# Weights by GpSimd's DMA queue, product operands in half tiles, and a reordered tail in a gated FNet/SwiGLU mix

## The chip, the cores and the metric

The kernel runs on one core of a Trainium2 chip, as one program and one launch. The metric is the device time in microseconds, from a handful of executions of the same program; the text gives the median and the range of the runs shown. The profile is of one execution. Its engines are TensorE (PE, with the weight loads as PEld), VectorE (DVE), ScalarE (ACT), GpSimd (POOL) and SyncE (SP). SP computes nothing here: it issues most of the DMAs, one after the other, and an issue that has to wait for a buffer holds up every issue behind it. GpSimd issues DMAs too, in the same in-order manner, between its few computations.

## The reference, cut to what matters

```python
def reference(x, dft_seq_re, dft_seq_im, dft_hid_re, dft_hid_im, w1, w3, w2, gate_w):
    g = sigmoid((x * gate_w).sum(-1, keepdims=True))
    # A: FNet mixing, the real part of a DFT along hidden and sequence
    a_re, a_im = x @ dft_hid_re.T, x @ dft_hid_im.T
    a = dft_seq_re @ a_re - dft_seq_im @ a_im
    # B: SwiGLU
    b = (silu(x @ w1) * (x @ w3)) @ w2
    return g * a + (1 - g) * b
```

The sequence has 2048 tokens, the hidden width D is 512 and the inner width F is 1376. All inputs are fp32. The DFT matrices are inputs, too: the kernel may use their symmetries only after it has compared the given matrices with themselves (a row against a representative row), and it holds a general path for matrices that lack them.

## The kernel before, in words

**Precision.** Every operand is split into a high and a low part (fp32r tiles of twice the size): `high` (L113) is a ScalarE copy that rounds, `low` (L116) a VectorE subtraction that keeps the rest. `mm3` (L127) multiplies high by high, high by low and low by high, so each product is three passes.

**Start, 0 to 17 us.** The first products go through four PSUM banks named C.

**Gate stage, 17 to 213 us.** The work is cut into items n = 0..21. An item is one chunk of 128 columns of F (11 chunks; the last is partial) for one half of the tokens: chunks 0 to 8 with the first half are n = 0..8, chunks 9 and 10 with both halves are n = 9..12, and chunks 0 to 8 with the second half are n = 13..21. `WSET[n]` names the weight set of an item; n = 9 and 10 share set 9, n = 11 and 12 share set 10, and the sets 11 to 19 are the chunks 0 to 8 a second time. In a Strassen-like form each item takes seven products of six matmuls each, into PSUM banks X, Y and Z. In program order an item issues X with operand 4 (and continues a bank that was started three items earlier), Z with 5, the first product of the item three ahead (`LOOK = 3`), X with 3, Z with 2, the second product of the item three ahead, and X with 6. The last three items have five products, as nothing is left to start.

For a weight set there are four tiles. `ws` holds the raw weights, loaded by `load_w` (L198) from `w13` (1024 columns wide, or 768 where the set's sums are not made again). `wa` (three operands) is split out of `ws` in the item four before its use. `wu` is four sums out of `ws` (`sums_wb`, L220 to L223). `wb` (four operands, 1 MB) is split out of `wu` by `high_wb` and `low_wb`, used in the item after, and for the chunks 0 to 8 written to DRAM (`wbsp`) by GpSimd's queue (L238), from where the sets of the second round read it back (`load_wb`, L205, SP's queue) instead of making it anew.

ScalarE's part of an item is: copy of X out of PSUM (`h`, L343), copy of Z (`u`, L347), copy of the early X (`s`, L261), the high parts, a silu (`h`, L376) and a silu on the gate (L279). VectorE adds X, Z and Y into these copies (L356, L364, L365, L380, L275), makes the sums and the low parts. The product h is written to DRAM (`hs`, L305) by GpSimd's queue.

**Work spread over the items.** Between these, the program places tasks from one queue by a table: `work(eng, us)` takes tasks of engine "D" (VectorE) or "A" (ScalarE) for about that many us at one of five points of an item (`early`, `ahead`, `second`, `mid`, `at_end`). Most of the tasks are the comparisons of the DFT matrices: a tile `t` of 128 by 1024 is loaded (L698), VectorE adds or subtracts the representative (`differ`, L703 to L709), ScalarE sums up the absolute values (`add_up`, L714), and the buffer is free again. Their loads stand on SP's queue in program order among the loads of `ws` and `wb`.

**H stage, 213 to 327 us.** The product with `w2` over 22 steps: `hr` is read back, split to `ht` (the `high_h`, `low_h` and `high_w2`, `low_w2` of the first steps stand in item 21), and eight PSUM banks are summed over 11 chunks, twice.

**DFT stage, 327 us to the end.** The products O1 (two), O2 and E2 (two) are made, split to `z_O` and `z_E`, and used by ten units Y0 to Y9 of 12 matmuls each (four O1 units, two O2 units, four E2 units). VectorE forms r out of Y, gate and B's part (L1271), four operations in an O1 or O2 unit and two in an E2 unit, and `out` is stored. Between them `verdict` (L543, L545) turns the sums of the comparisons into flags, a matmul with ones adds them up over the partitions in a PSUM pair named `count` (L548), and L549 writes a word that every engine loads at the end (L1285) to branch to the general path.

The order of all of this is written out by hand: the schedule is manual, and within an engine the instructions run in program order.

Of the kernel before, what the change touches and what calls it, by code (L numbers as in the profile page):

```python
# [30 lines left out]
def fnet_swiglu_gate_kernel(  # L31
# [108 lines left out]
    wbsp = dram.tile([NC, P, 2, 4, 256], F32, tag="wbsp", name="wbsp")  # L140
# [60 lines left out]
    def load_wb(w, spare=False):  # L201

        WB[w] = (parts(f"wb{w}") if spare else
                 wbp.tile([P, 2, 4, 256], F32R, tag="wb", name=f"wb{w}"))
        nc.sync.dma_start(WB[w].bitcast(F32), wbsp[SETS[w]])  # L205
# [10 lines left out]
    def sums_wb(w):  # L216
# [3 lines left out]
        nc.vector.tensor_add(u[:, 0], r[:, 3], r[:, 2])  # L220
        nc.vector.tensor_sub(u[:, 1], u[:, 0], r[:, 0])
        nc.vector.tensor_sub(u[:, 2], r[:, 0], r[:, 3])
        nc.vector.tensor_sub(u[:, 3], r[:, 1], u[:, 1])  # L223

    def wb_parts(w):
        return [(flat(WB[w][:, 0, i:j]), flat(WB[w][:, 1, i:j]), flat(WU[w][:, i:j]))
                for i, j in ((0, 2), (2, 4))]

    def high_wb(w):
        WB[w] = wbp.tile([P, 2, 4, 256], F32R, tag="wb", name=f"wb{w}")  # L230
        for v in wb_parts(w):
            high(*v[::2])

    def low_wb(w):
        for v in wb_parts(w):
            low(*v)
        if w < K:
            nc.gpsimd.dma_start(wbsp[w], WB[w].bitcast(F32))  # L238

    def prod(ps, n, wi, xi, start, chain=False):  # L240
        w = WSET[n]
        w, wi = (WA[w], wi) if wi < 3 else (WB[w], wi - 3)
        x = xo_at(ITEMS[n][1], xi)
        for q in range(2):
            sl = slice(q * P, (q + 1) * P)
            mm3(ps, w[:, 0, wi, sl], w[:, 1, wi, sl], x[:, 0, q, :], x[:, 1, q, :],
# [69 lines left out]

    def gate_up(n):
# [10 lines left out]
        if nw in WB or nw == 0:  # L328
            nw = None
        elif back(nw):  # L330
            load_wb(nw)
# [21 lines left out]
        if nw is not None and n > 1:  # L353
            high_wb(nw)
        prod(x, n, 3, 3, False, True)
# [4 lines left out]
        if nw is not None:  # L360
            low_wb(nw)
        run(mid, n)
# [23 lines left out]
    load_w(0, 0, 1)  # L386
# [1145 lines left out]
```

## Time and profile before

| what | us |
|---|---|
| median of 3 runs (lowest to highest) | 364.74 (364.08 to 364.97) |
| the profiled execution | 364.39 |
| its span, first to last instruction | 362.6 |
| PE busy | 350.2 (97%) |
| DVE busy | 310.8 (86%) |
| ACT busy | 234.4 (65%) |
| POOL busy | 60.6 (17%) |
| mean granted TensorE clock | 0.996 |

The profiled execution took 1.79 us more than its span, which lies before the first and behind the last instruction, and 0.35 us less than the median. In the views, a row of a timeline gives start and duration in us, engine, line, operation, tile written and tiles read, and in square brackets the idle time ahead of it with the instruction that ended it. A group of PE's matmuls has a modelled end, so the distance from one row's start to the next is the better measure of what a product takes. In the rows of waits the three numbers are the total in us, how often, and the longest. Buffer numbers are left out in the trace: `ws` is any `ws` tile.

### The profile page before, as it was taken

To read this page: it belongs to the slowest core of one execution; us is meant where nothing else is said; L and a number is where in the kernel's file an instruction comes from. 1 tells how busy PE (TensorE), PEld (TensorE's weight loads), DVE (VectorE), ACT (ScalarE), POOL (GpSimd) and SP (SyncE) were. 2 spreads that over 40 slices of the span, in tenths; PEclk is the share of its full clock that TensorE was granted. 3 is DMA by queue.
4 is the path that set the end of the run, shared out by engine and by line. 5 is a ranking of instruction groups with operands and counts; after the bars stand their busy time and mean duration, and the time that the engine had idled before them with its cause. 6 is when DMAs were issued, how large, how long until landed. Compare 5 with 4: busy or idle time off the path is not lost.

```text
span 362.6 us, 5086 instructions
## 1 busy us (share of the span) xinstructions
PE 350.2 (97%) x1720; PEld 303.5 (84%) x1720; DVE 310.8 (86%) x433; ACT 234.4 (65%) x394; POOL 60.6 (17%) x96
## 2 busy tenths in 40 slices
PE   7999999999999999999999989999999999999993
PEld 3888888888888777788888868888888888889983
DVE  3999989999779788778887679989889799997693
ACT  4876766656647577754433579354688999888630
POOL 0001212211110111111111553419011020000000
PEclk9999999999999999999999999999999999999998
DMA  7638967757537679999899519974969999996065
GB/s 243 277 136 308 360 243 263 288 217 275 202 118 246 229 216 409 405 360 417 311 389 304 193 71 377 409 281 139 349 223 338 398 410 409 411 407 235 2 261 207
DMA packets 32064, 102.77 MB, mean 283 GB/s; under 512 B 5666, under 2 KB 5923, under 8 KB 29988
## 3 DMA queue, kind: packets, MB, share of 16 engines
q1 hardware_dynamic: 27204, 81.96, 61.9%
q0 software_dynamic: 4832, 20.46, 14.5%
q8 instruction: 14, 0.23, 0.3%
q14 instruction: 14, 0.11, 0.1%
HBM read 77.76 MB, written 24.65 MB: 282 GB/s over the span
## 4 chain that ended last, share of the span: by engine, by line
PE 79%; DMA 6%; DVE 6%; ACT 5%; issue 2%; SPq 0%; DVEq 0%; ACTq 0%
PE H L127 31%; PE X L127 23%; PE Z L127 11%; PE Y L127 6%; DMA ws<-w 5%; PE C L127 3%; PE O L127 3%; DVE r L1271 2%; ACT t L714 2%; DMA xs_B<-xt 1%; PE Y L1246 1%; PE E L127 1%; DVE wb L116 1%; DVE t L703 1%; DVE h L364 1%
## 5 line engine op out<-in xcount | busy, mean ns | idle before, releaser
L127 PE MATMUL H<-w2t,ht 128*128 128x512 f32 (+1 forms) x528 | 114.1, 379 | 0.0
L127 PEld LDWEIGHTS H<-w2t,ht 128*128 128x128 f32 (+1 forms) x528 | 99.8, 189 | 14.2
L127 PE MATMUL X<-xo,wb 128*128 128x512 f32 x378 | 89.7, 381 | 3.5 <-DVE u L356 1.5
L127 PEld LDWEIGHTS X<-xo,wb 128*128 128x128 f32 x378 | 70.9, 189 | 16.1 <-ACT h L343 3.1
L714 ACT ACTIVATE t<-t 128x1024 f32<-128x1024 f32 (+1 forms) x68 | 67.5, 995 | 3.6 <-DVE t L703 2.3
L305 POOL DMA_DIRECT2D hs<-h x36 | 19.5, 543 | 103.2 <-DVE h L365 75.6
L703 DVE TENSOR_TENSOR t<-t,rep 128x1024 f32<-128x1024 f32 x28 | 33.2, 1217 | 0.0
L127 PE MATMUL X<-xo,wa 128*128 128x512 f32 x126 | 30.9, 380 | 0.2 <-DVE wa L116 0.2
L127 PE MATMUL Y<-xo,wa 128*128 128x512 f32 x126 | 30.6, 379 | 0.0
L127 PE MATMUL Z<-xo,wb 128*128 128x512 f32 x126 | 30.6, 379 | 0.0
L127 PE MATMUL Z<-xo,wa 128*128 128x512 f32 x126 | 30.6, 379 | 0.0
L356 DVE TENSOR_TENSOR u<-u,X 128x512 f32<-128x512 f32 x21 | 14.4, 685 | 17.5 <-PE X L127 12.9
L376 ACT ACTIVATE h<-X 128x512 f32<-128x512 f32 x21 | 12.4, 593 | 25.1 <-PE X L127 21.7
L113 ACT ACTIVATE wa<-ws 128x768 fp32r<-128x768 f32 (+2 forms) x21 | 17.0, 807 | 18.0 <-DMA ws<-w 12.4
L705 DVE TENSOR_TENSOR t<-t,rep 128x1024 f32<-128x1024 f32 x24 | 28.2, 1217 | 0.0
L113 ACT ACTIVATE ht<-hr 128x1024 fp32r<-128x1024 f32 x19 | 20.0, 1051 | 11.2 <-PE H L127 8.9
L127 PEld LDWEIGHTS X<-xo,wa 128*128 128x128 f32 x126 | 23.7, 189 | 3.9 <-DVE wa L116 0.6
L127 PEld LDWEIGHTS Y<-xo,wa 128*128 128x128 f32 x126 | 23.8, 189 | 3.4
L127 PEld LDWEIGHTS Z<-xo,wb 128*128 128x128 f32 x126 | 23.8, 189 | 3.4
L127 PEld LDWEIGHTS Z<-xo,wa 128*128 128x128 f32 x126 | 23.8, 189 | 3.4
L116 DVE TENSOR_TENSOR wa<-ws,wa 128x768 fp32r<-128x768 f32 (+1 forms) x22 | 19.3, 880 | 7.1 <-ACT wa L113 6.9
L116 DVE TENSOR_TENSOR ht<-hr,ht 128x1024 fp32r<-128x1024 f32 x19 | 23.1, 1218 | 1.3 <-ACT ht L113 1.2
(198 smaller groups left out, 487.2 us busy)
## 6 DMA issues: line engine op xcount, KB each, us to landing
t<-wt SPq DMA_DIRECT2D x60, 512.0 KB, 9.4
hr<-hs SPq DMA_DIRECT2D x19, 512.0 KB, 7.2
hs<-h POOLq DMA_DIRECT2D x36, 256.0 KB, 4.7
wbsp<-wb POOLq DMA_DIRECT2D x8, 1024.0 KB, 4.7
wb<-wbsp SPq DMA_DIRECT2D x8, 1024.0 KB, 9.3
ws<-w SPq DMA_DIRECT2D x11, 512.0 KB, 5.1
xr<-xw SPq DMA_DIRECT2D x8, 512.0 KB, 11.5
xs_B<-xt SPq DMA_DIRECT2D x7, 512.0 KB, 5.8
```

The source lines that it names most:

```text
L113: nc.scalar.activation(hi, src, AF.Copy)
L116: nc.vector.tensor_sub(lo, src, hi.bitcast(F32))
L127: nc.tensor.matmul(ps.rearrange("p (n a) -> p n a", a=2), u, turns(v)[:, some], **kw)
L305: nc.gpsimd.dma_start(hs[c][:, b * TB : (b + 1) * TB], h)
L356: nc.vector.tensor_add(u4, u4, x)
L364: nc.vector.tensor_add(u2, u2, z)
L376: nc.scalar.activation(g1, x, AF.Silu)
L703: nc.vector.tensor_sub(t, t, r)
L705: nc.vector.tensor_add(t, t, r)
L714: nc.scalar.activation(t[:, :n], t[:, :n], AF.Abs, accum_out=acc[:, i : i + 1])
L1246: nc.tensor.matmul(to, u[i], v[j], start=n == k == 0, stop=n == len(terms) - 1 and k == 2, skip_group_check=True)
L1271: nc.vector.scalar_tensor_tensor(rv[:, :, h], src, g_pos[:, k : k + 1], nv[:, :, h], op0=ALU.mult, op1=ALU.add)
```

## The change

1. **`load_w` by GpSimd's queue.** The sets 6 to 19 are loaded by GpSimd's queue, at points that a small table `NEXT_W` fixes: right behind `low_wb` of the set four before (in program order), or at the start of an item for the last ones. The sets 0 to 5 stay on SP.
2. **`wb` in two half tiles.** Half 0 holds the operands 4 and 5, half 1 the operands 3 and 6; each has two buffers, and `wbsp` is written and read by halves of 512 KB. For the sets that are read back, half 0 is loaded two items ahead, and half 1 at the start of the item ahead. The first sum made is now the one of `wu`'s third column block. The items 19 and 20 take a full spare tile as before.
3. **The table.** In the items 10 and 12 (where the next item has another set) the `mid` point places no VectorE task; before it placed one.
4. **Item 21.** `low_h(0)` and `low_w2(0)` move from `second` to `mid`, which stands behind the addition to u4.
5. **The tail.** E2's first product stands ahead of unit 0 and its second ahead of unit 4, where both stood ahead of unit 0. One `add_up` fewer stands between the two O1 products; `verdict` moves from unit 2 to behind unit 3's r; the sum of the flags goes to a corner of unit 7's own PSUM pair, and the word is written behind unit 7's r.

```diff
-    wbsp = dram.tile([NC, P, 2, 4, 256], F32, tag="wbsp", name="wbsp")
+    wbsp = dram.tile([NC, 2, P, 2, 2, 256], F32, tag="wbsp", name="wbsp")
-    def load_w(w, lo=0, hi=4):
+    def load_w(w, lo=0, hi=4, by=nc.gpsimd):
         if lo == 0:
             WS[w] = f4_a.tile([P, 4, 256], F32, tag=f"f4_{4 + w % (LOOK + 1)}", name=f"ws{w}")
-        nc.sync.dma_start(WS[w][:, lo:hi].rearrange("p a n -> p (a n)"),
-                          w13[SETS[w], :, lo * 256 : hi * 256])
+        by.dma_start(WS[w][:, lo:hi].rearrange("p a n -> p (a n)"), w13[SETS[w], :, lo * 256 : hi * 256])
+    def new_wb(w, half):
+        t = wbp.tile([P, 2, 2, 256], F32R, tag=f"wb{half}", name=f"wb{half}_{w}")
+        WB.setdefault(w, {})[half] = t
+        return t
+    def load_wb(w, half):
+
+        nc.sync.dma_start(new_wb(w, half).bitcast(F32), wbsp[SETS[w], half])
...
     def low_wb(w):
-        for v in wb_parts(w):
-            low(*v)
-        if w < K:
-            nc.gpsimd.dma_start(wbsp[w], WB[w].bitcast(F32))
+        for half in range(2):
+            low(*wb_parts(w, half))
+            if w < K:
+                nc.gpsimd.dma_start(wbsp[w, half], WB[w][half].bitcast(F32))
...
+    NEXT_W = {}
+    for w in range(LOOK + 3, len(SETS)):
+        v = w - LOOK - 1
+        at = (WSET.index(v) - LOOK, 0) if back(v) else (WSET.index(v) - 1, 1)
+        NEXT_W.setdefault(at, []).append(w)
...
-        if nw in WB or nw == 0:
+        if nw == 0 or nw == WSET[n] or len(WB.get(nw, ())) == 2:
             nw = None
         elif back(nw):
-            load_wb(nw)
+            load_wb(nw, 1)
             nw = None
...
-        elif wa not in WS:
-            load_w(wa, 0, 3 if back(wa) else 4)
-        w = WSET[min(n + LOOK + 2, last)]
-        if w - LOOK - 1 >= NC + 1 and w not in WS and w not in WA:
+        for w in NEXT_W.get((n, 0), ()):
             load_w(w, 0, 3)
...
             high_wb(nw)
+        if n + 2 < NI - 3 and back(WSET[n + 2]):
+            load_wb(WSET[n + 2], 0)
         prod(x, n, 3, 3, False, True)
         nc.vector.tensor_add(u4, u4, x)
...
             low_wb(nw)
+        for w in NEXT_W.get((n, 1), ()):
+            load_w(w, 0, 3 if back(w) else 4)
         run(mid, n)
...
-            do(mid, n, work, "D", 1.7 if n >= SPARE[1] else 1.3)
+            do(mid, n, work, "D", 1.7 if n >= SPARE[1] else 1.3 if WSET[n] == WSET[n + 1] else 0.0)
...
-        do(at_end if m else second, NI - 1, low_h, m)
-        do(at_end if m else second, NI - 1, low_w2, m)
+        do(at_end if m else mid, NI - 1, low_h, m)
+        do(at_end if m else mid, NI - 1, low_w2, m)
...
-                work("A", 2.4)
+                work("A", 1.2 if p else 2.4)
...
+    even(0)
     for u, (kind, za, zb, n, swap) in enumerate(UNITS):
+        if u == 4:
+            even(1)
         ps = next_two(f"Y{u}")
+        if u == 7:
+            sum_flags(ps)
...
         if u == 2:
             work_until(set(range(n_late)))
+        if u == 3:
             verdict()
-        if u == 6:
-            verdict_end(next_two("count"))
+        if u == 7:
+            see_flags(ps)
```

`even(p)` is the product E2 of half p and its split, which stood in a loop ahead of the units before.

How the instructions stand, at three places.

SP's queue in the items 8 to 12 before, where the loads of the comparison tiles `t`, of the weights `ws` and of `wb` take turns:

```order
L198 DMA ws12_1024<-w13 128x768
L698 DMA t38_1044<-wt 128x1024
L698 DMA t39_1046<-wt 128x1024
L698 DMA t40_1106<-wt 128x1024
L198 DMA ws13_1111<-w13 128x768
L698 DMA t41_1129<-wt 128x1024
L698 DMA t42_1181<-wt 128x1024
L198 DMA ws14_1190<-w13 128x768
```

and GpSimd's queue now, where the weights stand between the stores of `wb` (`wbsp`) and of h (`hs`); SP's queue keeps the comparison tiles:

```order
L248 DMA wbsp_97<-wb0_8_841 128x1024
L248 DMA wbsp_97<-wb1_8_843 128x1024
L198 DMA ws12_856<-w13 128x768
L320 DMA hs_96<-h7_805 128x512 x2
L198 DMA ws13_939<-w13 128x768
L320 DMA hs_96<-h8_891 128x512 x2
L320 DMA hs_96<-h9_972 128x512 x2
L198 DMA ws14_1094<-w13 128x768
```

The loads of the weights moved from between the comparison tiles to between the stores, and they are issued one to three items earlier in program order.

VectorE at the end of the gate stage before (item 21: `u4_21` is added to, and `ht0` and `w2t0` are the first operands of the H stage):

```order
L380 TENSOR_TENSOR h20_1794<-h20_1794,u4_20_1795 128x512
L116 TENSOR_TENSOR ht0_1864<-h19_1744,ht0_1864 128x1024
L116 TENSOR_TENSOR w2t0_1866<-w2r0_1791,w2t0_1866 128x512
L356 TENSOR_TENSOR u4_21_1845<-u4_21_1845,X21_1693 128x512
L364 TENSOR_TENSOR h21_1844<-h21_1844,Z21_1843 128x512
```

and now:

```order
L402 TENSOR_TENSOR h20_1822<-h20_1822,u4_20_1823 128x512
L376 TENSOR_TENSOR u4_21_1868<-u4_21_1868,X21_1718 128x512
L116 TENSOR_TENSOR ht0_1888<-h19_1770,ht0_1888 128x1024
L116 TENSOR_TENSOR w2t0_1890<-w2r0_1819,w2t0_1890 128x512
L386 TENSOR_TENSOR h21_1867<-h21_1867,Z21_1866 128x512
```

The two low parts moved from ahead of the addition to u4 to behind it.

VectorE in the DFT stage now, from the second half of O1's first split on (before, all the comparisons stood ahead of s0, and the four low parts of E2 ahead of r0):

```order
L116 TENSOR_TENSOR z_O10_3025<-s0_3021,z_O10_3025 128x1024
L736 TENSOR_TENSOR t62_2945<-t62_2945,rep3_2573 128x1024
L736 TENSOR_TENSOR t63_3005<-t63_3005,rep3_2573 128x1024
L1235 TENSOR_TENSOR s1_3069<-e1_3068,O1_1_3029 128x512
L1236 TENSOR_TENSOR s1_3069<-e1_3068,O1_1_3029 128x512
L116 TENSOR_TENSOR z_O11_3073<-s1_3069,z_O11_3073 128x1024
L116 TENSOR_TENSOR z_O2_3076<-O2_3077,z_O2_3076 128x1024
L116 TENSOR_TENSOR z_E2_3119<-E2_0_3120,z_E2_3119 128x258 x2
L1303 SCALAR_TENSOR_TENSOR r0_3153<-Y0_3140,tail_93,nb0_2933 128x2x128 x4
```

and on ScalarE, where E2's second split now stands behind seven sums of the comparisons (four before, which stood behind that split):

```order
L113 ACTIVATE z_E2_3119<-E2_0_3120 128x258 x2
L741 ACTIVATE t57_2887,tail_93<-t57_2887 128x1024
L741 ACTIVATE t58_2890,tail_93<-t58_2890 128x1024
L741 ACTIVATE t59_2902,tail_93<-t59_2902 128x1024
L741 ACTIVATE t60_2915,tail_93<-t60_2915 128x1024
L741 ACTIVATE t61_2925,tail_93<-t61_2925 128x1024
L741 ACTIVATE t62_2945,tail_93<-t62_2945 128x1024
L741 ACTIVATE t63_3005,tail_93<-t63_3005 128x1024
L113 ACTIVATE z_E2_3119<-E2_1_3225 128x258 x2
```

Two comparisons moved in between the two splits of O1, and E2's second split moved behind all sums.

More of the change, by code (lines that the diff above doesn't have):

```diff
@@ L193, in back, with load_kept @@
         return w >= NC and SETS[w] > 0
-    def load_w(w, lo=0, hi=4):
+    def load_w(w, lo=0, hi=4, by=nc.gpsimd):
         if lo == 0:
             WS[w] = f4_a.tile([P, 4, 256], F32, tag=f"f4_{4 + w % (LOOK + 1)}", name=f"ws{w}")
-        nc.sync.dma_start(WS[w][:, lo:hi].rearrange("p a n -> p (a n)"),
-                          w13[SETS[w], :, lo * 256 : hi * 256])
[L201 to L205, printed above, removed]
+        by.dma_start(WS[w][:, lo:hi].rearrange("p a n -> p (a n)"), w13[SETS[w], :, lo * 256 : hi * 256])
[5 more added lines that the diff above has]
+        nc.sync.dma_start(new_wb(w, half).bitcast(F32), wbsp[SETS[w], half])
+    KEPT = {}
+    def load_kept(w):
+        KEPT[w] = parts(f"wb{w}")
+        WB[w] = {half: KEPT[w][:, half].rearrange("p (h k) n -> p h k n", h=2) for half in range(2)}
+        for half in range(2):
+            nc.sync.dma_start(WB[w][half].bitcast(F32), wbsp[SETS[w], half])
     def wa_parts(w, lo, hi):
@@ L527, in fnet_swiglu_gate_kernel @@
     for n in (NI - 3, NI - 2, NI - 1):
-        do(mid, n - 2, load_wb, WSET[n], n < NI - 1)
         if n < NI - 1:
-            do(at_end, n, lambda w=WSET[n]: free(WB[w]))
+            do(mid, n - 2, load_kept, WSET[n])
+            do(at_end, n, lambda w=WSET[n]: free(KEPT[w]))
+        else:
+            for half in range(2):
+                do(mid, n - 2, load_wb, WSET[n], half)
     n = NI - 1 - LOOK
@@ L1224, in fnet_swiglu_gate_kernel @@
     work("D", 1.2)
-    t = yp.tile([P, 2, 2, 516], F32R, tag="z_E2", name="z_E2")
-    for p in range(2):
-        two = next_two(f"E2_{p}")
-        ps = two[:, :258], two[:, 512:770]
-        forms(*ps, ("E2",), range(2), p)
-        z = Z["E2", p] = t[:, p]
-        for v in range(2):
-            split(z[:, 0, 258 * v : 258 * v + 258], z[:, 1, 258 * v : 258 * v + 258], ps[v])
     def same_d(lo, hi):
```

59 lines of the change are left out of this document (36 added, 23 removed).

## The prediction

> **What bounds the kernel now.** I read the page first, for the busy shares.
>
> ```profile
> PE 350.2 (97%) x1720; PEld 303.5 (84%) x1720; DVE 310.8 (86%) x433; ACT 234.4 (65%) x394; POOL 60.6 (17%) x96
> ```
>
> PE sets the time. The change removes no matmul, so all it can win is PE's idle time: 12 us of the span of 362.6. The waits of PE say who causes the rest:
>
> ```profile
> PE X L127 <- DVE u L356: 1.5, 1, 1.5
> PE X L127 <- ACT h L343: 1.5, 4, 0.6
> PE X L127 <- DMA wb<-wbsp: 0.5, 1, 0.5
> ```
>
> Their sum understates it, since a pause costs a refill too. So I took PE's timeline of the gate stage and counted products.
>
> ```profile
> 105.25 2.75 PE L127 MATMUL X<-xo,wb 128*128 128x512 f32 x12
> ...
> 128.20 1.46 PE L127 MATMUL X<-xo,wa 128*128 128x512 f32 x6
> 130.11 1.56 PE L127 MATMUL X<-xo,wb 128*128 128x512 f32 x6 [0.46 <-ACT h L343]
> ...
> 146.00 1.56 PE L127 MATMUL X<-xo,wb 128*128 128x512 f32 x6 [0.48 <-DMA wb<-wbsp]
> ...
> 163.72 2.75 PE L127 MATMUL X<-xo,wb 128*128 128x512 f32 x12
> ...
> 172.78 2.75 PE L127 MATMUL X<-xo,wb 128*128 128x512 f32 x12
> ...
> 209.04 1.46 PE L127 MATMUL Z<-xo,wa 128*128 128x512 f32 x6
> 212.02 1.56 PE L127 MATMUL X<-xo,wb 128*128 128x512 f32 x6 [1.52 <-DVE u L356]
> 213.42 2.75 PE L127 MATMUL H<-w2t,ht 128*128 128x512 f32 x12
> ```
>
> ```profile
> 213.40:327.40 114.00, 114.00 (x530) 99.80 (x529) 107.18 (x122) 87.80 (x145) 24.09 (x21) 1.00 0.89 334
> ```
>
> An undisturbed item of seven products takes 172.78 − 163.72 = 9.06 us, 1.294 each. From 105.25 to 163.72 there are six items, 42 products: 58.47 − 54.36 = **4.1 us lost**. From 163.72 to 213.42 there are 37 products: 49.70 − 47.89 = **1.8 us lost**, all of it at 212.02. The last row is the H stage in the view by stretches (its first column is the length, its second PE's busy time): no pause there. Two causes, then, and the tail.
>
> The cause of the 4.1 is in the chain of waits, though it is not the engine that PE's wait names.
>
> ```profile
> 118.66 1.14 ACT t L714 x2
> ...
> 119.81 0.33 SPq L698
> ...
> 120.19 5.58 DMA ws<-w
> ...
> 136.01 10.84 DMA ws<-w
> ```
>
> A load of `ws` stood on SP behind a load of a comparison tile that waited for a buffer, which ScalarE's `add_up` (L714) frees. It was issued at 120.19, landed 5.6 us later, and ScalarE, which works in order, stood before the high part of `wa`:
>
> ```profile
> 125.80 0.84 ACT L113 ACTIVATE wa<-ws 128x768 fp32r<-128x768 f32 x1 [3.38 <-DMA ws<-w]
> 129.47 0.60 ACT L343 ACTIVATE h<-X 128x512 f32<-128x512 f32 x1
> 146.94 0.85 ACT L113 ACTIVATE wa<-ws 128x768 fp32r<-128x768 f32 x1 [3.88 <-DMA ws<-w]
> ```
>
> The copy out of X at 129.47 is late by this wait, and PE's next X at 130.11 with it. An idle of 3.4 us of ScalarE costs PE 130.11 − 128.20 − 1.29 = 0.6 us: the rest is slack.
>
> **The change part by part.** *Weights by GpSimd's queue (4.1 us at stake).* It takes the loads of `ws` out of the line behind the comparison tiles, and issues those of sets 13 and 14 an item or more earlier. What they now stand behind are stores of h and of `wb`.
>
> ```profile
> ws<-w SPq DMA_DIRECT2D x11, 512.0 KB, 5.1
> ws<-w SPq DMA_DIRECT2D x9, 384.0 KB, 8.2
> hs<-h POOLq DMA_DIRECT2D x36, 256.0 KB, 4.7
> ```
>
> With PE undisturbed, the item of set 14's load (n = 10) begins near 115.6 and its `mid` stands about five products in, at 122; with the 10.8 us of the slowest load above it lands at 133, while item 12 wants it about 8 us after its start near 133.7, at 141. Set 15 is the closest: issued in item 12 near 140, wanted in item 13 near 150.8; with the median of 8.2 it has 2.6 us left, with 10.8 none. So the 4.1 go but for one late load, which costs by the rows above up to 0.6 with a chance of a half: **3.8 gained**. The 0.48 us at 146.00, where `wb` came late, is in the 4.1: in half tiles, with one half issued two items ahead, the half of operands 4 and 5 has an item more, and the other (512 KB) is issued where the 1 MB was. Each of GpSimd's issues takes 0.54 us of a queue that is 17% busy; 14 loads and 8 more stores are 12 us there, hidden beside all else. One `differ` less at `mid` in the items 10 and 12
>
> ```profile
> L703 DVE TENSOR_TENSOR t<-t,rep 128x1024 f32<-128x1024 f32 x28 | 33.2, 1217 | 0.0
> ```
>
> takes 1.2 us from VectorE where its item is fullest; two comparisons of the small tiles fall into the H stage for it, about 1.3 us of VectorE under a PE that never waits there. Bounds of this part: 4.1 (no load late) to 0 (first rival).
>
> *Item 21 (1.8 us at stake).* The addition to u4 has its copy of Z at 208.55 and its X when PE goes on to Z at 209.04, but stands behind two low parts whose high part comes late.
>
> ```profile
> 207.95 0.60 ACT L347 ACTIVATE u<-Z 128x512 f32<-128x512 f32 x1 [0.64 <-PE Z L127]
> 208.44 1.05 ACT L113 ACTIVATE ht<-h 128x1024 fp32r<-128x1024 f32 x1
> 209.52 1.23 DVE L116 TENSOR_TENSOR ht<-h,ht 128x1024 fp32r<-128x1024 f32 x1 [1.95 <-ACT ht L113]
> 210.67 0.70 DVE L116 TENSOR_TENSOR w2t<-w2r,w2t 128x512 fp32r<-128x512 f32 x1
> 211.29 0.67 DVE L356 TENSOR_TENSOR u<-u,X 128x512 f32<-128x512 f32 x1
> ```
>
> Moved ahead, it runs from 209.25 to 209.9 in the idle 1.95, before Z's product ends at 210.3; X follows at once and H could start at 211.63. Late next are the two low parts: ScalarE has a sum of the comparisons (about 1 us) that may fall ahead of the high part of `ht`, so low `ht` runs from 210.2 to 211.35 and low `w2t` to 212.0, where the third matmul of H wants it at about 212.06. I leave 0.3 for that: **1.5 gained**. Bounds: 1.8, and 0.7 if H waits a full low part (1.1).
>
> *The tail (sign open).* Rows of now:
>
> ```profile
> 333.38 1.23 DVE L116 TENSOR_TENSOR z_O<-s,z_O 128x1024 fp32r<-128x1024 f32 x1 [1.13 <-ACT z_O L113]
> 335.93 0.69 DVE L1208 TENSOR_TENSOR s<-e,O 128x512 f32<-128x512 f32 x1 [1.33 <-ACT e L1207]
> 338.35 1.23 DVE L116 TENSOR_TENSOR z_O<-s,z_O 128x1024 fp32r<-128x1024 f32 x1 [1.13 <-ACT z_O L113]
> 343.10 1.05 ACT L714 ACTIVATE t<-t 128x1024 f32<-128x1024 f32 x1
> 343.58 4.78 DVE L1271 SCALAR_TENSOR_TENSOR r<-Y,tail,nb 128x256 f32<-128x256 f32 x12
> 352.06 4.49 PE L1246 MATMUL Y<-dt,z_E 128*128 128x260 f32 x36 [0.64 <-DVE r L1271]
> 356.59 0.88 DVE L1271 SCALAR_TENSOR_TENSOR r<-Y,tail,nbr 128x256 f32<-128x256 f32 x2 [0.46 <-PE Y L1246]
> ```
>
> In the times of now: behind low z_O (ends 334.6) come two comparisons of 1.2, so s starts at 337.0 rather than 335.93, the second low z_O at 339.4, z_O2's at 340.6, and the two low parts of E2's first product end near 342.6; r0 starts there, 1.0 earlier than 343.58, as two of the four low parts of E2 are not ahead of it. Sixteen r's at 4.78/12 = 0.40 end at 349.0. The seven sums on ScalarE, 1.04 each from about 341.9, end at 349.2; the verdict (0.5), which reads them, and E2's second low parts follow to about 350.8; the other sixteen r's take 6.4 and end at 357.2, against 356.59 + 0.88 = 357.47. PE's last E2 units start at 350.8 and need 4 × 4.49/3, to 356.8, with the last r's 0.9 behind: 357.7. Two ends either side of now: I take **0**, with bounds of 0.5 gained and 1.5 lost.
>
> Sum: 3.8 + 1.5 + 0 = 5.3 off 364.39, the profiled execution: 359.1. That execution is 0.35 under the median, so 359.4; I write **359.5**. All bounds at their good end give 364.74 − 6.4 = 358.3.
>
> **The rivals.** *One: the loads stay late, because bandwidth and not the queue was what they waited for.* For it: the DMA share where the stalls are,
>
> ```profile
> 130.00:157.00 27.00, 25.54 (x113) 21.14 (x114) 22.06 (x30) 18.66 (x36) 3.25 (x6) 1.00 1.02 378
> ```
>
> full at 378 GB/s, and the 10.84 us for 384 KB at 136.01. Against it: an earlier issue adds 10 us of room, and at 120.19 the load landed in 5.6 and was late all the same. If the 4.1 stay: 364.74 − 1.5 = 363.2. The Trainium skill ("DMA: Bandwidth & Descriptors", section on issuing engines not being separate DMA queues) says that DMAs of all engines run on the same 16 DMA engines, and that issuing from several saves only issue time, which would give this rival's time. The trace agrees that the engines are full there; but what the chain shows ahead of the load at 120.19 is the issue, SP's wait at L698 for ScalarE.
>
> *Two: the tail loses.* E2's second split stands behind seven sums on ScalarE, each after its comparison, and the last two comparisons' tiles are loaded late. It decides once the seventh sum ends after 349.2: each us from there is one on PE's and VectorE's last units. At 1.5 to 2.5 us: 361 to 362. For it: the chain has no slack by my walk. Against: VectorE is done with the last comparison at 337.0, 12 us earlier.
>
> *Three, the other side: GpSimd's queue makes loads late where they were not.* Set 6 to 12 now wait for `low_wb` and its stores.
>
> ```profile
> 41.66 0.54 POOL L238 DMA_DIRECT2D wbsp<-wb  x1 [3.47 <-DVE wb L116]
> 50.02 0.84 ACT L113 ACTIVATE wa<-ws 128x768 fp32r<-128x768 f32 x1
> ```
>
> The load follows the store, at 42.8, and lands by 47.9 with the 5.1 of its size: 2.1 us in hand. If it took some 5 us longer on this queue, beside the stores, ScalarE would idle 3 us as at 125.80 and PE lose 0.6 per set; from nine late sets on (9 × 0.6 = 5.4) the whole gain is gone, and with all 14 the time is 364.74 − 1.5 − 4.1 + 14 × 0.6 = 367.5. Against: h's stores land in 4.7 us from the same queue. The Trainium skill ("SBUF — State Buffer", on two separate sides) warns that GpSimd cannot write descriptors while VectorE holds their shared port in some operations. By that rule these loads would be late; the issues of 0.54 us with VectorE 86% busy show no sign of it.
>
> **How the numbers follow.** The sum as forecast: 0.72, own range 358.4 to 361. Rival one 0.10 at 363.2, two 0.10 at 361 to 362, three 0.08 at 364.5 to 367.5. The range of 358.4 to 362.6 leaves out three and most of one. A measurement here can tell about 0.3%, 1.1 us, from no change. Forecast and rival two are faster; rival one is 1.5 under and counts for half as no change; three is slower but for 0.02. Faster 0.87, no change 0.07, slower 0.06.
>
> **What would show it.** After the change ScalarE's waits for `ws` should be gone, the six items from 105 take 54.5 us, the last X of the gate stage start without a wait for u, and the last r end as long after H's start as now (357.47 − 213.42 = 144.05). Waits of `wa` on `ws` before 105 would be rival three, after 130 rival one; a wait of z_E or the verdict on ScalarE's sums is rival two. I am wrong if PE idles in the gate stage at other places, which a full VectorE could bring.

## The result, and the profile after

The changed kernel takes 361.46 us in the median of 8 executions (360.14 to 362.74), the kernel before 364.44 in the median of 8. The ratio is 0.992, with a 95% interval of 0.9898 to 0.9942: 2.9 us faster (2.1 to 3.7). The forecast was faster, 359.5 us, 5.3 us off the profiled execution's time. The direction holds, and a little more than half of the forecast gain arrived. The profiled execution took 362.30 us, 0.84 above this median, so the stages read from it explain the 2.1 us between the two profiled executions (spans 362.6 and 360.5 us), and not the whole 2.9.

The waits of PE after the change, in the same view as before:

```profile
PE Y L1263 <- DVE z_O L116: 0.8, 1, 0.8
PE C L127 <- ACT xo L113: 0.6, 2, 0.4
PE X L127 <- ACT h L398: 0.3, 1, 0.3
PE X L127 <- DMA wb<-wbsp: 0.2, 1, 0.2
```

Both waits that the change was to remove are gone, the 1.5 us for u and the 1.5 us on ScalarE's copies of X. The first line is new, and it lies in the tail; the 0.3 us for h is the wait of the row at 46.91 below. PE's timeline of the gate stage:

```profile
45.15 1.46 PE L127 MATMUL Z<-xo,wb 128*128 128x512 f32 x6
46.91 1.64 PE L127 MATMUL X<-xo,wa 128*128 128x512 f32 x6 [0.31 <-ACT h L398]
48.59 1.56 PE L127 MATMUL X<-xo,wb 128*128 128x512 f32 x6
49.99 1.46 PE L127 MATMUL Z<-xo,wa 128*128 128x512 f32 x6
...
106.97 2.75 PE L127 MATMUL X<-xo,wb 128*128 128x512 f32 x12
...
161.79 2.75 PE L127 MATMUL X<-xo,wb 128*128 128x512 f32 x12
...
208.41 1.46 PE L127 MATMUL X<-xo,wb 128*128 128x512 f32 x6
209.70 5.47 PE L127 MATMUL H<-w2t,ht 128*128 128x512 f32 x23
```

The rows from 106.97 to 161.79 are the six items that took 58.47 us before. They take 54.82 now, 3.65 less, and the last X follows Z without a pause. But PE reached the first of these rows later than before (106.97 against 105.25): 0.94 us were lost anew from 45 to 50 us, and the start took 0.64 longer. That 0.64 carries no meaning: over all the executions profiled in this study, whose start is nearly the same program, the first X began anywhere from 16.85 to 17.87 us.

To compare runs from here on, "gate loss" is the sum over PE's rows, from the first X to the first H, of what the distance to the next row's start has above 0.216 us per matmul (the 9.06 us of an undisturbed item over its 42 matmuls), where this surplus is over 0.08. "Tail" is the time from the first O matmul to the end of the last r, and "end" the time from there to the end of the span.

| us | before | after | difference |
|---|---|---|---|
| gate loss | 5.85 | 1.42 | −4.43 |
| H stage, first H to first O | 113.97 | 114.31 | +0.34 |
| tail | 30.08 | 30.73 | +0.65 |
| end | 5.13 | 5.76 | +0.63 |

With the 0.64 of the start, the sum is −2.17, the spans' difference (2.1) but for the small delays that gate loss leaves out. The gate stage gave what was forecast of it less one late weight set; the tail and the end took 1.3 us of that back. The prediction's own sign for the tail, the time from H's start to the last r, should have stayed at 144.05 us and is 145.04.

VectorE's timeline of the tail says where, after the change and, for the first s, before:

```profile
321.19 6.89 DVE L736 TENSOR_TENSOR t<-t,rep 128x1024 f32<-128x1024 f32 x6
328.00 0.68 DVE L1235 TENSOR_TENSOR s<-e,O 128x512 f32<-128x512 f32 x1
...
331.54 2.35 DVE L736 TENSOR_TENSOR t<-t,rep 128x1024 f32<-128x1024 f32 x2
333.81 0.68 DVE L1235 TENSOR_TENSOR s<-e,O 128x512 f32<-128x512 f32 x1
...
339.70 6.35 DVE L1303 SCALAR_TENSOR_TENSOR r<-Y,tail,nb 128x256 f32<-128x256 f32 x16
346.65 0.24 DVE L568 SCALAR_TENSOR_TENSOR tail<-tail 128x80 f32<-128x80 f32 x1 [0.59 <-ACT t L741]
```

```profile
330.96 0.69 DVE L1208 TENSOR_TENSOR s<-e,O 128x512 f32<-128x512 f32 x1 [0.31 <-ACT e L1207]
```

The first O matmul is at 324.01 (327.39 before). VectorE comes to s 4.0 us behind it without having waited, so it is late by itself (before, 3.6 us behind, and it had waited 0.31 for ScalarE). Then two more comparisons stand between the two s, and the verdict waits 0.59 us for ScalarE's seventh sum: this is the sign of rival two, at a smaller price than it was given.

### The profile page after: what moved, and what is told of

It reads as the page before. It is cut to its first block, busy times and chain, and to the rows that moved or that the text cites. A ratio compares the mean times of both kernels' runs of the same rounds, so it can differ in the third digit from the quotient of the medians.

```text
span 360.5 us, 5136 instructions
## 1 busy us (share of the span) xinstructions
PE 350.8 (97%) x1720; PEld 303.6 (84%) x1720; DVE 310.0 (86%) x433; ACT 234.2 (65%) x394; POOL 102.8 (29%) x118
## 4 chain that ended last, share of the span: by engine, by line
## 5 line engine op out<-in xcount | busy, mean ns | idle before, releaser
L127 PE MATMUL X<-xo,wb 128*128 128x512 f32 x378 | 88.8, 379 | 0.2 <-DMA wb<-wbsp 0.2
L765 POOL TENSOR_SCALAR mov_E<-mov_E 128x2 fp32r<-128x2 f32 x2 | 35.4, 17697 | 22.3 <-DVE mov_E L116 22.3
L248 POOL DMA_DIRECT2D wbsp<-wb x16 | 8.8, 553 | 57.5 <-DVE wb L116 56.7
```

Source lines behind the costliest of these rows:

```text
L127: nc.tensor.matmul(ps.rearrange("p (n a) -> p n a", a=2), u, turns(v)[:, some], **kw)
L248: nc.gpsimd.dma_start(wbsp[w, half], WB[w][half].bitcast(F32))
L765: nc.gpsimd.tensor_scalar(MV[kind][:, :, par, 128], MV[kind][:, :, par, 0].bitcast(F32), 1.0 - 2.0 * par, None, op0=ALU.mult)
```

## The experiments

Twelve kernels were run. Each is compared with the kernel before in executions on the same chip. In the diffs a line of "..." stands for what is left out.

### One part at a time: item 21, and the tail

Item 21's part alone, on the kernel before:

```diff
-        do(at_end if m else second, NI - 1, low_h, m)
-        do(at_end if m else second, NI - 1, low_w2, m)
+        do(at_end if m else mid, NI - 1, low_h, m)
+        do(at_end if m else mid, NI - 1, low_w2, m)
```

> The kernel before with one edit: in the last item the two low parts (ht0, w2t0) stand behind the addition to u4. Theory (the forecast's second term): PE's wait for u at the last X of the gate stage goes (1.52 us idle, 1.8 us with the refill), H loses about 0.3 in its first matmuls; the time falls by 1.5 us, to 362.9. The profile after showed H's start 0.3 us longer, so 1.3 to 1.6. Rival: the 1.8 is only handed on, to the first low part that H needs (1.1 us) and to VectorE in the H stage, and 0.7 us or less is left.

Measured: 362.72 against 364.03 us, ratio 0.9959 (0.9944 to 0.9973), so 1.5 us faster (1.0 to 2.0). PE's wait for u is gone, and the H stage takes 114.04 us, only 0.07 more than before. The forecast's second term is right in size.

The tail alone, on the kernel before:

```diff
-                work("A", 2.4)
+                work("A", 1.2 if p else 2.4)
...
-        ps = two[:, :258], two[:, 512:770]
-        forms(*ps, ("E2",), range(2), p)
...
+    even(0)
     for u, (kind, za, zb, n, swap) in enumerate(UNITS):
+        if u == 4:
+            even(1)
...
+        if u == 3:
             verdict()
```

> The kernel before with the new tail alone (E2's second product ahead of unit 4, verdict behind unit 3, the flags' sum in unit 7's bank). Theory one: the new tail is a loss by itself, since E2's second split waits behind seven sums on ScalarE; from H's end to the last r 30.6 us rather than 30.1, the whole 0.5 us slower. Theory two: the loss seen after the change came from VectorE's surplus out of the H stage (its comparisons ended 0.4 us later against H's end) and the tail by itself is even or 0.2 better. The forecast had 0, between 0.5 better and 1.5 worse.

Measured: 363.52 against 364.03 us, ratio 0.9981 (0.9969 to 0.9994): 0.7 us faster (0.2 to 1.1). The tail is 29.18 us against 30.08. Theory one is out; by itself the new tail is a gain of 0.9 us in its stage. The end is 5.63 us against 5.13; these are single executions, and over the ten kernels of this study without the smaller table, the kernel before among them, the end lies anywhere from 4.59 to 5.68. In the full change the same tail takes 30.73. So something ahead of the tail costs it 1.5 us there.

### What costs the tail: the table

The changed kernel with the table of before:

```diff
-            do(mid, n, work, "D", 1.7 if n >= SPARE[1] else 1.3 if WSET[n] == WSET[n + 1] else 0.0)
+            do(mid, n, work, "D", 1.7 if n >= SPARE[1] else 1.3)
```

> The changed kernel with the table as before (one VectorE task at mid in the items 10 and 12 too). After the change VectorE ended its comparisons 0.8 us later against H's end than in the kernel before with the new tail alone, and from H's end to the last r it took 30.7 against 29.2 us. Theory: the smaller table hands two comparisons (2.4 us) from the gate stage to H and to the tail, and the tail pays 1.5 us for it; here the tail is 29.2 again. The gate stage may lose up to 0.5 by a full VectorE in the items 10 and 12. Time 0.5 to 1 us less than after the change (360.5 to 361). Rival: VectorE's surplus is of no account, the gate stage stalls again in the items 10 to 12 and the time is 362 or more.

Measured: 359.27 us against 364.08, ratio 0.9876 (0.9851 to 0.99). That is 4.5 us under before where the change as it stands is 2.9 under: the smaller table alone costs about 1.6 us, from ratios whose intervals just touch. A second pair below differs in the table alone, too (0.9912 with the smaller table, 0.9873 with the one of before), and there the intervals are apart, at 1.4 us. The tail of this run on VectorE:

```profile
317.17 9.17 DVE L736 TENSOR_TENSOR t<-t,rep 128x1024 f32<-128x1024 f32 x8
326.66 0.69 DVE L1235 TENSOR_TENSOR s<-e,O 128x512 f32<-128x512 f32 x1 [0.32 <-ACT e L1234]
...
330.65 0.69 DVE L1235 TENSOR_TENSOR s<-e,O 128x512 f32<-128x512 f32 x1 [0.36 <-ACT e L1234]
...
336.88 6.35 DVE L1303 SCALAR_TENSOR_TENSOR r<-Y,tail,nb 128x256 f32<-128x256 f32 x16
343.15 0.23 DVE L568 SCALAR_TENSOR_TENSOR tail<-tail 128x80 f32<-128x80 f32 x1
```

All eight last comparisons now stand ahead of the first s, which waits for ScalarE as before, and none between the two s. The first O matmul is at 323.09, so the first r comes 13.8 us behind it, against 15.7 in the changed kernel, and the verdict has nothing to wait for. The tail is 29.18, as with the new tail alone. In the gate stage the full VectorE of item 10 costs 0.9 us at 119 to 122 (gate loss 1.66 in all, with 0.5 at 45 to 50):

```profile
119.35 1.13 PE L127 MATMUL X<-xo,wa 128*128 128x512 f32 x4 [0.21 <-DVE wa L116]
```

So a slot of 1.2 us that is left empty in the items 10 and 12 saves 0.9 us of PE there, and costs 1.5 in the tail, where VectorE sets the pace. The last r's of the two kernels, the changed one first, differ too:

```profile
353.06 1.68 DVE L1303 SCALAR_TENSOR_TENSOR r<-Y,tail,nbr 128x256 f32<-128x256 f32 x4
```

```profile
350.04 0.88 DVE L1303 SCALAR_TENSOR_TENSOR r<-Y,tail,nbr 128x256 f32<-128x256 f32 x2 [0.42 <-PE Y L1263]
351.39 0.88 DVE L1303 SCALAR_TENSOR_TENSOR r<-Y,tail,nbr 128x256 f32<-128x256 f32 x2 [0.47 <-PE Y L1263]
```

In the changed kernel VectorE is behind PE and makes the last four in one go; with the table of before it waits for PE, and the last two pairs start 1.35 us apart.

### Is it the queue, the place, or the half tiles?

The weights alone by GpSimd's queue, on the kernel before (with `NEXT_W`, and wb in one tile):

```diff
-    def load_w(w, lo=0, hi=4):
+    def load_w(w, lo=0, hi=4, by=nc.gpsimd):
...
+        for w in NEXT_W.get((n, 1), ()):
+            load_w(w, 0, 3 if back(w) else 4)
         run(mid, n)
```

> The kernel before with the first part alone: loads of the weights by GpSimd's queue at the new points; wb in one tile, table, item 21 and tail as before. Theory: this part carries the gate stage's gain. From the first X to the first H 196.2 us before, 191.9 after the change, of which item 21 is 1.8 to 2.8; so 193 to 194 here (3 us off, less what a late set 6 costs), and the time 361.5 to 362 with H and tail as before. Rival: without the smaller table and the half tiles VectorE is too full in the items 10 and 12 and wb comes late, and no more than 1 us is left (363).

Measured: 364.37 against 364.08 us, ratio 1.0009 (0.9993 to 1.0026): no gain at all. The 3 us that this part was to carry did not come. ScalarE's waits for the weights behind 100 us are gone as forecast, but the gate loss is 7.03, more than before. PE's timeline:

```profile
146.70 2.47 PE L127 MATMUL X<-xo,wb 128*128 128x512 f32 x6 [1.99 <-DMA wb<-wbsp]
148.96 2.28 PE L127 MATMUL Z<-xo,wb 128*128 128x512 f32 x6
151.08 1.46 PE L127 MATMUL X<-xo,wa 128*128 128x512 f32 x6
```

The 1 MB of `wb` was issued at 135.50 (135.59 before) and lands at 146.7 (146.0 before), so PE, held up less ahead of it, waits 1.99 us rather than 0.48. Behind the pause PE loses more. The same place by stretches (length, PE's busy time, granted clock, DMA share, GB/s):

```profile
144.60:146.70 2.10, 0.11 (x2) 1.00 1.00 412
146.70:148.90 2.20, 2.20 (x6) 0.61 1.02 415
148.90:151.00 2.10, 2.10 (x7) 0.59 1.05 431
151.00:153.00 2.00, 2.00 (x11) 1.00 1.04 394
```

After the pause the granted clock is 0.6 for 4.3 us, and the two products take 2.2 us each rather than 1.3. These 1.8 us are those of the profiled execution, which at 366.19 us was 1.8 above the median; without them its gate loss would be 5.25, 0.6 less than before, and in the medians no gain is left of that.

The half tiles alone, on the kernel before (`new_wb`, `load_wb` by halves, half 0 two items ahead; weights on SP as before):

```diff
+        if n + 2 < NI - 3 and back(WSET[n + 2]):
+            load_wb(WSET[n + 2], 0)
         prod(x, n, 3, 3, False, True)
```

> The kernel before with the second part alone: wb in two half tiles, one loaded two items ahead; weights on SP at the old points, table, item 21 and tail as before. Theory: weights and halves need each other. Before, PE lost 4.1 us from 105 to 163 (0.6 for wb, the rest behind late weights); with the weights alone it lost 5.2 there, 3.9 of it at the first wb that is read back. Halves alone leave the waits for the weights (0.84 at 119 and 120, 0.7 at 130, 0.9 at 140, 0.5 at 150) and take the 0.6 to 0.7 at 146: 3.2 lost, the time 0.7 us under before. Rival: the halves free the DMA engines or SP's line for the weights too, the loss is under 1.5 and the time 2 us or more under before.

Measured: 364.74 against 364.12 us, ratio 1.0011 (0.9998 to 1.0024): no gain either. The wait for `wb` is gone, but the weights are as late as before. ScalarE's timeline has the waits:

```profile
126.07 0.84 ACT L113 ACTIVATE wa<-ws 128x768 fp32r<-128x768 f32 x1 [3.28 <-DMA ws<-w]
136.71 0.84 ACT L113 ACTIVATE wa<-ws 128x768 fp32r<-128x768 f32 x1 [3.33 <-DMA ws<-w]
148.16 0.84 ACT L113 ACTIVATE wa<-ws 128x768 fp32r<-128x768 f32 x1 [4.14 <-DMA ws<-w]
```

Both together, on the kernel before (the two diffs above; table, item 21 and tail as before):

> The kernel before with the first and the second part together; table, item 21 and tail as before. Theory: with both, the loss from 105 to 163 us is the 0.9 of a full VectorE at 119 and 120 alone, and that of set 6 at 46 (0.5 to 0.9): the time 2.3 to 2.7 us under before, where the weights alone gave nothing and the halves alone 0.7 at most. Rival: the two add up, each with its own gain, and the sum is that of the two single runs (about 0.5 us).

Measured: 362.07 against 364.12 us, ratio 0.9936 (0.9922 to 0.9951): 2.3 us faster (1.8 to 2.8), from two parts that give nothing singly. Without the pause for u (2.1 in this run) the gate loss is 2.1: 0.9 at 119 to 122, and 0.5 where H begins. The profiled execution (364.26) was the slowest of the seven; its H stage of 115.24 us begins with a stretch at a lower clock, shown at the end. The rival, that the parts add up, is out. The pair, item 21 and the tail do add up: 0.64%, 0.41% and 0.19% off the time make 1.24%, and 0.9876 is what the change without its table measured.

All the changed kernel's weights back on SP's queue, at the new places in program order:

```diff
-    def load_w(w, lo=0, hi=4, by=nc.gpsimd):
+    def load_w(w, lo=0, hi=4, by=nc.sync):
```

> The changed kernel with all loads of the weights back on SP's queue, at the places in program order that the change gave them; half tiles, table and tail as changed. Theory queue: the weights must not stand behind comparison loads that wait for a buffer; on SP they do again, ScalarE waits for ws in the items 9 to 12 and PE loses the 4 us again, 365 us. Theory point: what helped is that each load is issued earlier in program order (set 13 and 14 by one and two items), SP's order alone would do; then ScalarE's waits stay under 1 us and the time is 361, with the first set on this queue early enough too (no wait for set 6).

Measured: 361.95 against 364.08 us, ratio 0.9944 (0.9924 to 0.9964); the change has 0.992 (0.9898 to 0.9942). Theory queue forecast 365 and falls; theory point forecast 361. Behind the start, ScalarE waits once for weights, 0.87 us, and behind 100 us PE loses 0.14. What it lost lies at 48.44, and that has another cause, an h buffer whose store had not ended:

```profile
47.79 0.60 ACT L361 ACTIVATE h<-X 128x512 f32<-128x512 f32 x1 [3.34 <-DMA hs<-h]
48.44 1.56 PE L127 MATMUL X<-xo,wb 128*128 128x512 f32 x6 [1.26 <-ACT h L361]
```

So it is the place in program order that brought the weights early, not the engine that issues them: at the new places SP sends them early enough, too, though it still waits for the buffers of comparison tiles in between.

### The one late set

After the change ScalarE waits once more for weights, in item 2. Its row, GpSimd's issue of that set, and what SP sent meanwhile:

```profile
45.53 0.84 ACT L113 ACTIVATE wa<-ws 128x768 fp32r<-128x768 f32 x1 [2.90 <-DMA ws<-w]
```

```profile
34.55 1.14 POOL L248 DMA_DIRECT2D wbsp<-wb  x2 [8.97 <-DVE wb L116]
35.68 0.54 POOL L198 DMA_DIRECT2D ws<-w  x1
36.48 0.55 POOL L320 DMA_DIRECT2D hs<-h  x1 [0.26 <-DVE h L387]
```

```profile
28.03 3.69 SPq L174 DMA_DIRECT2D xs_B<-xt  x4
31.82 0.38 SPq L714 DMA_DIRECT2D rep<-wt  x1
32.24 0.55 SPq L725 DMA_DIRECT2D t<-wt  x1
```

Set 6, issued at 35.68, was there 9.8 us later. SP, which no longer waits for weight buffers, sent a representative row at 31.82 that went at 58.65 before, and a comparison tile behind it. Two experiments on the changed kernel, the first with set 6 back on SP, the second with those two loads sent later:

```diff
-    for w in range(LOOK + 3, len(SETS)):
+    for w in range(LOOK + 4, len(SETS)):
...
+        if n == 2:
+            load_w(6, by=nc.sync)
```

> The changed kernel with set 6 alone loaded by SP at the start of item 2, as before the change. After the change set 6 landed 9.7 us after its issue on GpSimd's queue and ScalarE waited 2.9 us for it, and PE's two next X products started 0.46 and 0.39 us late. Theory: that one late set costs 0.9 us; the wait goes, the time falls by 0.9 us, to 360.6. Rival: it is a disturbance of the one profiled execution, and the time does not change.

```diff
-        nc.sync.dma_start(held[kind], wt[16 * g])
+        (nc.gpsimd if g == 2 else nc.sync).dma_start(held[kind], wt[16 * g])
...
-        nc.sync.dma_start(TR[i][:, : src.shape[-1]], src)
+        (nc.gpsimd if i == 33 else nc.sync).dma_start(TR[i][:, : src.shape[-1]], src)
```

> The changed kernel, set 6 where the change put it, but the first representative row and the first comparison tile (1 MB together) are loaded by GpSimd's queue at their place in program order (items 5 and 7), where SP, no longer held by the weights, sent them at 31.8 us. Theory traffic: set 6 was late because these two loads ran ahead into the busy stretch from 30 to 45 us; then it lands in 5 to 6 us of its issue, ScalarE's wait of 2.9 us falls below 0.5 and the time by up to 0.9. Theory queue: set 6 is late for the two stores of wb (1 MB) that stand right ahead of it in the same queue; then it still lands 9 us or more after its issue, and the time does not change.

Measured: set 6 on SP 361.23 us, ratio 0.9927 (0.9909 to 0.9944), gate loss 0.32; the two loads later 360.83 us, ratio 0.9912 (0.9895 to 0.993), gate loss 0.12. In the profile both do what was expected: the wait is gone. In the second, the stores of `wb` stand ahead of set 6 in GpSimd's queue as they did, and the set is in time: issued at 35.72, and ScalarE's row waits for PE, not for the load.

```profile
42.82 0.85 ACT L113 ACTIVATE wa<-ws 128x768 fp32r<-128x768 f32 x1 [0.15 <-PE Y L127]
```

So it was the traffic and not the queue. Nor was it a disturbance of one execution, as the first run's rival has it: ScalarE's wait, 2.5 to 2.9 us, is in the profiles of all four kernels with set 6 on GpSimd's queue and those two loads at their early place, and in none of the other ten. What it cost PE differs: 0.94 us in the changed kernel, 0.49 with the table of before, 0.17 and nothing in the two kernels with the new places and the old tail. In the time neither repair is separated from the change (0.9898 to 0.9942), whose executions range over 2.6 us, so the 0.9 us of the profiled execution was not confirmed as a gain.

### Versions that beat both

The changed kernel with the table of before, the two loads later, and the verdict behind unit 5's r:

```diff
-        if u == 3:
+        if u == 5:
             verdict()
```

> The changed kernel with three edits: first representative and first comparison tile by GpSimd's queue at their place in program order (no late set 6), the table as before the change, and verdict behind unit 5's r rather than unit 3's (its 0.5 us on VectorE then stands behind E2's second low parts). Theory: gate stage 190.5, tail 29 at most, sum 1.4 + 1.7 us less than after the change in the stages, some of which the stores of out take back at the end (5.1 to 6.6 us from the last r to the end): 359 to 360. Rival: the stores of out bound the end whatever the last r does, and the time stays at 360.5 to 361.

Measured: 360.19 against 364.08 us, ratio 0.9892 (0.987 to 0.9914). The tail is 30.68, not 29. The sum of the flags stands in PE's queue ahead of unit 7, and it needs the verdict:

```profile
348.48 0.19 PE L573 MATMUL Y<-const-float32-1.0,tail 128*1 128x1 f32 x2 [1.43 <-DVE tail L570]
348.60 4.30 PE L1263 MATMUL Y<-dt,z_E 128*128 128x260 f32 x36
```

The same with the verdict where the change put it:

> The changed kernel with the first representative and the first comparison tile by GpSimd's queue and the table as before the change; verdict where the change put it. Theory: in the run with verdict behind unit 5 the flags' sum, ahead of unit 7 on PE, waited 1.4 us for verdict, and the tail gave back 1.5 us; here the tail is 29.2, the gate stage 191.9 (1.4 lost at 119 to 122), the time 358.6 to 359.3, equal to the table alone or up to 0.6 better, by set 6. Rival: verdict's place is of no account and the tail stays at 30.7.

Measured: 359.68 against 364.12 us, ratio 0.9873 (0.9854 to 0.9892); the tail is 29.18 again, so the verdict's place was the cause. Not better than the table alone (0.9876).

And with item 10's comparison moved to item 11:

```diff
-            do(mid, n, work, "D", 1.7 if n >= SPARE[1] else 1.3 if WSET[n] == WSET[n + 1] else 0.0)
+            do(mid, n, work, "D", 1.7 if n >= SPARE[1] else 0.0 if n == 10 else 2.4 if n == 11 else 1.3)
```

> As the run before it, with the task of item 10's mid moved to item 11's mid (two there, where the next item has the same weight set and VectorE makes no sums), so that VectorE is not full in item 10 and no comparison is handed on to H. Theory: the stall at 119 to 122 goes (0.9 us) and the tail stays 29.2: 357.8 to 358.5. Rival: VectorE is as full in the items 11 and 12, or a comparison's tile has not landed there, and the 0.9 comes back at another place.

Measured: 359.66 against 364.12 us, ratio 0.9876 (0.9859 to 0.9894). The stall at 119 is gone, and its rival came true: 1.2 us are lost in item 12, the next one that makes a new set.

```profile
137.43 1.13 PE L127 MATMUL X<-xo,wa 128*128 128x512 f32 x4 [0.35 <-DVE wa L116]
138.89 1.56 PE L127 MATMUL X<-xo,wb 128*128 128x512 f32 x6 [0.33 <-ACT h L361]
```

The four versions that leave no VectorE task of the gate stage to the end lie between 0.9873 and 0.9892 and are not told apart; the simplest, the change without its table, is 4.5 us faster than the kernel before.

## Why the prediction was right, and where it was not

**The gate stage.** The forecast of 3.8 us from 105 to 163 us came out as 3.65, and the sign that it named (54.5 us for the six items) as 54.82. That the size fits is in part luck, as the 4.1 us at stake had more causes than the one that it was given to. First, 0.9 of it, at 119 to 122, is no wait for a load: PE waits there for a low part of VectorE, the weights and the half tiles together leave it in place, and the smaller table removes it. The prediction named no gain for the table. Second, it took the rest for the weights', with 0.48 for `wb` inside it; the runs show that the weights by themselves give nothing, as PE then waits 2 us for `wb`, and the half tiles by themselves give nothing either. The step that failed is the reading that each wait has a price of its own: two transfers were late by about the same time, and only the pair is worth 2.3 us. Third, it named two remedies for the weights, another queue than SP's and an earlier issue, and led with the queue; on SP at the new places the loads are early too. The Trainium skill ("DMA: Bandwidth & Descriptors", section on issuing engines not being separate DMA queues) says that another issuing engine saves no more than issue time. The runs agree with that sentence, 0.9944 on SP and 0.992 on GpSimd with overlapping intervals; but the time that the first rival drew from it, 363.2, did not come, for the order was changed as well as the engine.

**Rival three, in one set.** It named the right place, early weights behind stores on GpSimd's queue, and its margin of 2.1 us was worked out for the wrong set: the store at 41.66 and the use at 50.02 belong to set 7. For set 6 the issue is at 35.68 and the use at 42.6. That left 6.9 us, more than the 5.1 that such a load took before, and still it was late by 2.9: the prediction asked what the weights would stand behind on the new queue, and not what SP would send sooner once it was free of them. Its price in the profile was 0.94 us, not 0.6. The other thing that this rival named, issues of GpSimd held up by VectorE, did not show: the 14 issues of `ws` there took 0.54 us each in the mean.

**Item 21.** Forecast 1.5, measured alone 1.5 (1.0 to 2.0). In the full change H's first matmuls cost 0.34, where 0.3 was left for them.

**The tail and the table.** The forecast was 0. By itself the new tail wins 0.7 us, and the full change loses 0.65 in the tail and 0.63 at the end. The step that failed is the sentence that two comparisons fall into the H stage "under a PE that never waits there". PE does not wait there, and that was not the question: VectorE's tasks are in a fixed order up to the tail, where VectorE and not PE sets the pace, so work put off from the gate stage is paid at the end. The prediction's walk through the tail did count the two comparisons between the two s, and it had the second s right (337.2 in its times, which are those of the kernel before, against a forecast of 337.0); but it began with a VectorE as punctual as before. The first s came 0.4 us later, r0 at 343.1 rather than 342.6, and the last r at 358.1 rather than 357.7, where before it was 357.5.

Over all the kernels, the two stages sort by the tail and the table:

| us | tail | end |
|---|---|---|
| new tail with the smaller table (4 kernels) | 30.67 to 30.73 | 5.76 to 6.61 |
| new tail without it (5) | 29.18, and 30.68 with the verdict late | 4.59 to 5.68 |
| old tail without it (5) | 30.07 to 30.08 | 4.98 to 5.50 |

So the smaller table costs 1.5 us in the tail, 0.85 at the end (the means are 6.10 and 5.25) and 0.2 in the H stage (114.24 to 114.31 against 113.97 to 114.12, but for the one execution with the lower clock), and saves 0.9 to 1.4 in the gate stage. That makes 1.15 to 1.65, and the two pairs measured 1.6 and 1.4. This is the largest part of the missing 2.4 us (5.3 forecast, 2.9 measured). The seven sums on ScalarE (rival two) hold VectorE up for 0.59 us in it, and not at all once VectorE is in time.

**The time.** The 361.46 us lie outside the sum's own range (358.4 to 361) and within rival two's (361 to 362), but not for that rival's reason: the tail was slow by VectorE's late comparisons, and the sums on ScalarE were the smaller part. That the measured time lies within 358.4 to 362.6 is owed to the room that the range has for losses, not to a tail that was understood.

**What stays open.** The end is the landing of the last stores of `out`: those of 512 KB landed 2.8 us after their issue before, and 4.1 after the change (medians). It is not the new tail as such, as the table above shows, and it goes with the smaller table, under which the last four r's come in one go. Whether this bunching is what makes the stores land late was not tried.

## What to carry to other kernels

A wait that ends last hides the one right behind it: ask what else is due at the same time, and test the parts of a change together as well as apart. A loader that is freed from one queue sends other loads sooner, so count those in the stretch they move into. Work that is put off in program order "under" the bounding engine is paid where its own engine takes over the pace; look at the last stage before calling it hidden.

## What the hardware showed that was not expected

A pause of PE of 1.99 us (weights alone, before 146.70) was followed by 4.3 us at a granted clock of 0.6, and one of 1.86 us (weights and halves together, before 210.38) by a stretch at 0.50, while four pauses of 1.52 us (before, at 212.02), 1.53 (the tail alone), 1.57 (weights alone, at 213.68) and 1.83 us (halves alone) left it at 1.00. The second, by stretches:

```profile
210.30:212.20 1.90, 1.82 (x6) 0.77 0.69 250
212.20:214.30 2.10, 2.10 (x6) 0.50 0.00 0
```

In the first case the two products behind the pause cost 1.8 us more, about the pause's own length again. Both fell in executions that were about 2 us slower than their kernel's median (366.19 against 364.37, 364.26 against 362.07), so it need not happen in every execution. The Trainium skill ("TensorE: Matmul & The Clock Gate", section "Why this matters for your kernels") advises against gaps of over some 3 us; here the clock fell behind shorter ones in two of six cases.

An operation of GpSimd on 128 by 2 elements, 1.1 us long before, took 35 us in the changed kernel, for as long as VectorE ran comparisons and low parts with two operands in SBUF without a pause:

```profile
292.97 35.19 POOL L765 TENSOR_SCALAR mov_E<-mov_E 128x2 fp32r<-128x2 f32 x1 [22.33 <-DVE mov_E L116]
```

It ended 6 us ahead of its use and cost nothing here. It took as long in all four kernels with the smaller table, and 1.1 us in the ten others. The Trainium skill ("SBUF — State Buffer", section "SBUF: two separate sides") says that the two engines share ports, and that an operation of VectorE with two inputs in SBUF can lock out one of GpSimd that reads SBUF, for the whole instruction. The row fits that in kind, but one comparison takes 1.2 us, and what holds GpSimd over so many of them was not tried.
